# A gated mix of a spectral filter and a Mish layer: constants on another queue, Mish called first, half of the FFT result added on VectorE, and a new order

## The chip, the cores and the metric

The kernel runs on one core of a Trainium2 chip. The metric is device time in microseconds (us), the median of three runs; beside it stands one profiled execution with its own time and its span from the first to the last instruction.

## What is computed

```python
def reference(A_x, A_w_r, A_w_i, B_x, B_w1, B_b1, B_w2, gate_w):
    x = A_x                                             # (1, 2048, 512), bf16
    g = sigmoid((x * gate_w).sum(-1, keepdims=True))
    X = rfft2(x.astype(float32)) * (A_w_r + 1j * A_w_i)
    a = irfft2(X, s=(2048, 512)).astype(bfloat16)
    h = x @ B_w1 + B_b1                                 # 512 -> 1792
    b = (h * tanh(softplus(h))) @ B_w2                  # Mish, 1792 -> 512
    return g * a + (1 - g) * b
```

## The kernel before

The 2048 rows are 16 tiles of 128 rows (row p*16 + t belongs to tile t), in four chunks of four tiles. All work is a graph of named tasks. A written list, ORDER, names every task once; each engine, and each DMA queue, runs its own tasks in the order of that list. A token is name:engine:slot. The engine is given where several could do the task; the slot is the PSUM bank (of eight; tasks with pairs take two) or the temporary (of three). A task waits for its data and for all users of the slot's last owner. So order and slots are fixed by hand or by a planner outside the kernel, and TensorE never runs ahead of a task that waits. DMAs are in the lists too: most are issued by SP, a few by ScalarE (ACT) between its own instructions.

The tasks, with the lines of the profile:

- Loads (L462): x0, x2, x4, x8, x12 (tiles from that number on, 256 or 512 KB), w1_0, w1_4, w1_8, w2_2, w2_8, w2_0 (weights of the two layers), wr and wi pieces (spectral weights, named by half and piece: wi0s1), cRF and cFD (transform constants, both kept where w2's first two blocks come later), ldM and ldG (c_m and c_g, constants of the row transform), xt8 to xt15 (tiles transposed by the DMA, L461).
- tr0 to tr7: transposes of x tiles on TensorE (L560), copied to xT by evx (L492 on VectorE, L495 on ScalarE). tr_b does it for the bias and gate vectors (braw, graw).
- FFT forward: bf adds and subtracts the halves of x (L573), p (L586, needs cRF), its evacuation ep, d (L601, needs cFD and all p), its evacuation ed, then sixteen DMAs s (rE from rD, after all ed), then t (L716) and its evacuation et.
- Filter, in eight groups q: sw swaps halves (L726 VectorE, L727 ScalarE), p1, p2 and ad multiply and add (L734, L737, L740). The spectral weights are spread by wrm and wim (L640 ACT, L642 and L643), wrn and win (L660, L653), and small tasks wrc, wic, wrz, wiz. An edge column goes through e1 (L756), es, xp, ead, e2, e3.
- FFT backward: it (L794) and its evacuation eit, eight DMAs hx (rC from rF), id (L838), ec (L845, L846) and ey (L849), which leave yb, the result without its last matmul.
- First layer: m c_f (chunk c, block f; four 512-column matmuls, L864) and the Mish h c_f on ScalarE (L869). Chunks 2 and 3 write into rD and rS, so h2 waits for the s DMAs and h3 for all wrm and wim.
- Second layer: n t (fourteen matmuls, L882). In the kernel before, every n is followed in the same bank by ip (L890), the last FFT matmul, with constants RFs that are already scaled by exp of the gate's argument; o (L896, L899) scales the sum by omg = 1 - g. The scaled constants come by gate, zcl, ez (a power on POOL, L698), ezb, zt (L815), zte, the DMAs zw and zr through HBM, and rfs (L821).

The parameter merge says for how many tiles the FFT part is instead added behind the second layer: for t below merge, n has no ip in its bank, ip goes to a bank of its own with unscaled constants, and fin computes

```python
e.scalar_tensor_tensor(out=bs[:, t, :], in0=bank(b), scalar=gcol[:, t:t + 1],
                       in1=bs[:, t, :], op0=ALU.mult, op1=ALU.add)
```

on VectorE, after o; gcol is g, computed by one more small task, gc. Before, merge is 0. Results go out in pairs of tiles (out1, out3 and so on).

Of the kernel before, what the change touches and what calls it, by code (L numbers as in the profile page):

```python
# [9 lines left out]
F32 = mybir.dt.float32  # L10
AF = mybir.ActivationFunctionType
# [312 lines left out]


ORDER = """
warm::0 ebase ones graw x0 ident wrp0 wrp1 cRF x2 braw w1_0 tr1::0 bf0_0:dve bf0_1:dve tr0::1 evx1:act x4 p0::2 evx0:dve tr2::0 bf2_1:dve tr3::1
bf2_0:dve evx2:act p1 evx3:dve tr_b::4 x8 p2::6 p3 ep0:dve m0_0::5 ep2:act ev_b m0_2::1 ldM1 h0_0 bf4_1:dve tr7::0 h0_2 tr6::4 evx7:dve m0_3::5 wi0s2
bf4_0:dve evx6:act x12 tr4::1 bf8_1:dve h0_3 p6::6 p4::2 bf8_0:dve p5 evx4:act p7 tr5::5 xt11 ep4:act ep6:dve m0_1::4 cFD p8::0 p9 w1_4 evx5:dve h0_1
p10::6 p11 gate0::5 ep8:act bf12_1:dve bf12_0:dve m1_2::4 wi0s1 ep10:act zcl0 wip1 p12::0 ez0 h1_2 p14::2 p13 p15 ezb0 wip0 ep12:act m1_0::6 ez10 wi0s0  # L330
ep14:dve m0_6::7 h1_0 wr0s1 omg0 d6::2 h0_6 d7 d14::0 d15 ed6:act d10::4 ed14:dve d0::6 d1 wr0s0 d11 ed0:act m0_7::2 wim011:dve wr0s2 ed10:act d12::0
wim010:dve d13 d4::6 w1_8 d5 ed12:act wim001:dve m1_5::3 ed4:dve d2::4 h0_7 d3 wrm011:pool d8::0 h1_5 d9 ldM0 m1_6::2 ed2:dve ed8:act m1_7::3 h1_6 s1_1
wrm000:dve m1_4::0 wrm010:act s1_3 wim000:dve s0_3 m0_9::2 wrm001:dve s1_0 m0_11::1 win0:dve h1_4 s1_2 h1_7 m0_12::4 s0_1 wrn0:dve h0_11 s0_0 m1_10::3
h0_9 ldM3 h0_12 wic0:dve t3_0::0 t3_1 h1_10 wiz0:dve wrc0:pool t2_0::6 s3_3 et3:dve t2_1 m0_8::4 et2:act s3_1 m0_13::5 wrz0:dve s0_2 sw3_1:dve:0 h0_8
sw2_1:dve:1 s3_0 m1_13::6 sw3_0:dve h0_13 s3_2 sw2_0:dve p2_3:dve m0_5::7 wi1s0 h1_13 p2_2:dve t1_0::4 xt9 h0_5 t0_0::0 p1_3:dve t0_1 m1_1::6 et0:act
p1_2:dve wi1s1 ad_3:dve t6_0::2 t6_1 h1_1 t7_0::0 sw0_0:dve:2 t7_1 et6:act m0_10::7 ad_2:dve xt8 sw0_1:dve et7:act t1_1 sw6_0:dve:1 m1_9::6 p2_0:dve
h0_10 wr1s0 m1_3::0 sw7_0:dve:0 h1_9 p1_0:dve s2_2 m1_11::1 et1:act wim100:dve xt10 ad_0:dve m1_8::6 wim111:act sw6_1:dve m1_12::7 sw1_0:dve:2 wr1s1
sw1_1:dve wim101:dve m0_4::4 h1_12 p1_1:dve s2_3 h1_8 m2_3::5 wim110:dve s2_1 h1_11 m2_13::6 h0_4 p2_1:dve s2_0 h1_3 win1:dve ldM2 m2_8::7 m2_6::4 xt14
wrm101:dve wrm110:act m2_10::0 ad_1:dve h2_8 edge wrm100:dve m2_9::1 h2_13 xt15 wrm111:dve m2_7::7 h2_10 wic1:dve h2_6 wrn1:dve xt12 m2_1::0 h2_7 h2_3
m2_12::4 sw7_1:dve xt13 h2_1 wrc1:dve t4_0::6 wrz1:dve wiz1:pool t4_1 h2_12 t5_0::2 p2_6:dve t5_1 et4:act ldG1 m2_2::0 p2_7:dve p1_7:dve et5:act  # L340
m2_0::4 rft sw4_1:dve:2 inv m2_11::5 h2_9 sw4_0:dve ad_7:dve w2_8 h2_0 m3_5::1 p1_4:dve sw5_0:act:0 p2_4:dve m3_10::4 h2_11 sw5_1:dve ldG0 m3_8::2
p1_6:dve h3_5 h3_10 ad_4:dve m2_4::1 h3_8 ldG2 ad_6:dve m3_4::4 h2_2 p2_5:dve h2_4 p1_5:dve m3_3::5 ldG3 h3_4 ad_5:dve m3_12::1 h3_3 w2_2 e1::0 m3_7::5
h3_12 xp1::0 es0::1 m3_2::1 es1 h3_7 xp2 gate8::0 ead::2 h3_2 e2::5 m2_5::1 zcl8 e3 ez8 it0_0::4 ez18 h2_5 it0_1 ezb8 omg8 it6_0::2 zt::0 it4_0::6
eit0:act zte it6_1 it4_1 zw eit6:dve it3_0::0 it3_1 eit4:act it1_0::4 it1_1 eit1:dve eit3:act it7_0::2 it7_1 it5_0::6 zr it5_1 eit7:act it2_0::0 w2_0
eit5:dve it2_1 m3_0::4 eit2:act m3_13::5 h3_0 hx0_01 rfs m3_6::0 h3_13 hx0_11 hx0_00 m3_11::1 h3_6 hx0_10 m3_9::5 h3_11 hx4_00 m3_1::4 hx4_11 h3_9
id0::0 h3_1 hx4_10 id1 id2::6 ec0:act:2 id3 hx4_01 ec2:act:0 ey0_1 ey2_1 ey0_0 n0_0::4 ey2_0 n2_0::5 id8::6 id6::0 id9 n3_0::2 ec8:dve:0 ey8_0 ey8_1
ip3_0 id12::6 o3_0:dve id13 id7 ec12:act:0 n1_0::3 ec6:act:2 ey12_1 ey6_1 ey6_0 ey12_0 id10::0 id11 ip1_0 ec10:act:0 id14::6 o1_0:dve n6_0::2 ey10_0
ey10_1 ip6_0 ip0_0 o6_0:act ip2_0 o0_0:dve n8_0::0 o2_0:act out1 out3 n9_0::1 n7_0::5 ip8_0 n11_0::4 o8_0:dve id15 n10_0::0 ec14:act:0 ey14_1 ey14_0
n12_0::6 ip7_0 ip12_0 o7_0:act ip11_0 o12_0:dve id4::2 id5 o11_0:act n15_256::7 out7 ec4:act:0 ey4_0 ip9_0 ey4_1 n5_0::6 o9_0:act out9 ip10_0 ip15_256
ip5_0 o10_0:dve o15_256:act n4_0::1 o5_0:act out15_256 out11 n13_0::0 ip13_0 ip4_0 o13_0:dve n14_0::6 o4_0:act out13 out5 ip14_0 n15_0::7 o14_0:act  # L350
out14 ip15_0 o15_0:act out15_0
"""


def _build(nc, A_x, A_w_r, A_w_i, B_x, B_w1, B_b1, B_w2, gate_w, out, merge=0, xtp=8, NWARM=13):
# [8 lines left out]
    G = _Graph(3)  # L364
    es = ExitStack()
    with es:
        def sb(name, shape, dt):
            return es.enter_context(nc.sbuf_tensor(name, shape, dt))
# [48 lines left out]
        cst = w2_sb[:, 0, :]  # L417
        RF = w2_sb[:, 1, 0:128]
# [30 lines left out]
        def new_sem(name):  # L449
            return es.enter_context(nc.semaphore(name))  # L450
# [171 lines left out]
        for ri, (dstv, nm) in enumerate(((Wr, "wr"), (Wi, "wi"))):  # L622
# [3 lines left out]
            for fh in range(2):  # L626
# [5 lines left out]
                      writes=[(nm, fh, "p")], deps=dp)  # L632
# [180 lines left out]
        if merge < NT:  # L813
# [8 lines left out]
                out=RFs[:, merge:NT, :], in0=RFs[:, merge:NT, :], in1=RFT.unsqueeze(1).to_broadcast([128, NT - merge, 128]), op=ALU.mult))],  # L822
# [147 lines left out]
```

## Time and profile before

| | |
|---|---|
| runs | 145.08, 145.98, 146.22 us; median 145.98 |
| profiled execution | 145.54 us, span 143.8 us, mean granted clock 0.975 |
| TensorE | 130.7 us busy (91%), 918 matmuls |
| weight load / VectorE / ScalarE / POOL | 72.1 / 74.7 / 78.0 / 7.7 us |
| DMA | 20.67 MB, 144 GB/s on the mean |

The slices of the span are 3.6 us each, one digit per slice, in tenths. A line of the waits gives an instruction, what it waited for, the sum in us, how often, and the longest. The chain is the series of work that ended last, in order of time: start, length, what. Matmuls overlap, so the spacing in a run of them, not the mean duration of one, is what a matmul takes.

### The profile page before, as it was taken

To read this page: it belongs to the slowest core of one execution; us is meant where nothing else is said; L and a number is where in the kernel's file an instruction comes from. 1 tells how busy PE (TensorE), PEld (TensorE's weight loads), DVE (VectorE), ACT (ScalarE), POOL (GpSimd) and SP (SyncE) were. 2 spreads that over 40 slices of the span, in tenths; PEclk is the share of its full clock that TensorE was granted. 3 is DMA by queue.
4 is the path that set the end of the run, shared out by engine and by line. 5 is a ranking of instruction groups with operands and counts; after the bars stand their busy time and mean duration, and the time that the engine had idled before them with its cause. 6 is when DMAs were issued, how large, how long until landed. Compare 5 with 4: busy or idle time off the path is not lost.

```text
span 143.8 us, 2316 instructions
## 1 busy us (share of the span) xinstructions
PE 130.7 (91%) x918; PEld 72.1 (50%) x918; DVE 74.7 (52%) x125; ACT 78.0 (54%) x107; POOL 7.7 (5%) x16
## 2 busy tenths in 40 slices
PE   7499963999969999899997999999999999999992
PEld 5356733864526434353466645555444444644451
DVE  0566740799795999989736626067520212222100
ACT  3269970699966997999968973003130010412021
POOL 3000230050100000000022000000000000000000
PEclk9959998699999999999999999999999999999999
DMA  4999997006999989559980667000030000122031
GB/s 116 326 417 212 189 209 294 9 0 146 220 271 130 187 133 234 147 168 318 319 305 1 219 271 310 7 0 0 5 143 5 0 0 0 58 92 91 0 146 55
DMA packets 15710, 20.67 MB, mean 144 GB/s; under 512 B 5780, under 2 KB 11796, under 8 KB 15636
## 3 DMA queue, kind: packets, MB, share of 16 engines
q1 hardware_dynamic: 15232, 20.30, 53.2%
q10 hardware_dynamic: 468, 0.23, 0.6%
q8 instruction: 7, 0.11, 0.4%
q14 instruction: 3, 0.02, 0.1%
HBM read 13.19 MB, written 2.10 MB: 106 GB/s over the span
## 4 chain that ended last, share of the span: by engine, by line
PE 57%; DVE 14%; ACT 12%; DMA 10%; issue 3%; POOLq 1%; ACTq 0%; POOL 0%
PE ps L882 34%; PE ps L864 10%; DMA w_sb<-c_front 10%; ACT hs L869 4%; DVE tmp L726 3%; PE ps L838 3%; ACT rD L495 3%; PE ps L890 2%; PE ps L601 2%; DVE rC L740 2%; DVE tmp L737 2%; PE ps L794 1%; DVE rC L734 1%; ACT rW L640 1%; PE ps L716 1%
## 5 line engine op out<-in xcount | busy, mean ns | idle before, releaser
L864 PE MATMUL ps<-rX,w_sb 128*128 128x512 bf16 x224 | 52.8, 384 | 1.2 <-ACT rD L869 0.4
L864 PEld LDWEIGHTS ps<-rX,w_sb 128*128 128x128 bf16 x224 | 21.1, 99 | 26.0 <-issue 2.3
L882 PE MATMUL ps<-w_sb,hs 128*128 128x512 bf16 x112 | 25.3, 379 | 0.0
L899 DVE TENSOR_SCALAR rX<-ps,omg 128x512 bf16<-128x512 f32 x7 | 5.3, 750 | 25.5 <-PE ps L890 25.5
L869 ACT ACTIVATE hs<-ps,b1f 128x512 bf16<-128x512 f32 x28 | 17.9, 691 | 0.9 <-PE ps L864 0.5
L896 ACT ACTIVATE rX<-ps,omg 128x512 bf16<-128x512 f32 (+1 forms) x10 | 6.1, 642 | 21.4 <-PE ps L890 21.4
L845 ACT ACTIVATE tmp<-ps 128x512 f32<-128x512 f32 x7 | 4.0, 596 | 24.2 <-PE ps L838 24.1
L882 PEld LDWEIGHTS ps<-w_sb,hs 128*128 128x128 bf16 x112 | 10.8, 98 | 12.1
L849 DVE TENSOR_TENSOR rA<-tmp,ps 128x512 bf16<-128x512 f32 x16 | 10.1, 682 | 8.0 <-ACT tmp L845 7.9
L495 ACT ACTIVATE rC<-ps 128x1024 bf16<-128x1024 f32 x12 | 12.2, 1052 | 3.1 <-PE ps L716 1.9
L882 PE MATMUL ps<-w_sb,rS 128*128 128x512 bf16 (+1 forms) x70 | 12.9, 336 | 0.0
L882 PE MATMUL ps<-w_sb,rD 128*128 128x512 bf16 x56 | 12.6, 379 | 0.0
L869 ACT ACTIVATE rS<-ps,b1f 128x512 bf16<-128x512 f32 x14 | 9.4, 692 | 0.9 <-PE ps L864 0.9
L869 ACT ACTIVATE rD<-ps,b1f 128x512 bf16<-128x512 f32 x14 | 8.7, 710 | 1.9 <-PE ps L864 1.9
L882 PEld LDWEIGHTS ps<-w_sb,rS 128*128 128x128 bf16 x70 | 6.8, 98 | 5.5
L601 PE MATMUL ps<-w_sb,rC 128*128 128x128 bf16 x64 | 5.7, 264 | 3.7 <-DMA w_sb<-c_front 3.7
L882 PEld LDWEIGHTS ps<-w_sb,rD 128*128 128x128 bf16 x56 | 5.4, 98 | 6.4
L573 DVE TENSOR_TENSOR rB<-rA 128x1024 bf16<-128x1024 bf16 (+1 forms) x10 | 5.4, 578 | 4.9 <-DMA rA<-in_A_x_dram 4.9
L495 ACT ACTIVATE rD<-ps 128x1024 bf16<-128x1024 f32 x5 | 4.9, 1024 | 5.2 <-PE ps L601 5.2
L601 PEld LDWEIGHTS ps<-w_sb,rC 128*128 128x128 bf16 x64 | 5.3, 121 | 4.7 <-issue 4.2
L726 DVE COPY tmp<-rC 64x1024 bf16<-64x1024 bf16 x15 | 6.1, 420 | 1.8 <-ACT rC L495 1.4
L586 PE MATMUL ps<-w_sb,rB 128*128 128x128 bf16 x64 | 5.2, 236 | 1.9 <-DMA w_sb<-c_front 1.9
(79 smaller groups left out, 126.3 us busy)
## 6 DMA issues: line engine op xcount, KB each, us to landing
w_sb<-in_B_w_dram SPq DMA_DIRECT2D x3, 768.0 KB, 10.5
rF<-c_m SPq DMA_DIRECT2D x4, 512.0 KB, 8.1
rE<-rD SPq DMA_DIRECT2D x16, 128.0 KB, 4.7
rB<-c_g SPq DMA_DIRECT2D x4, 512.0 KB, 7.9
out_dram<-rX SPq DMA_DIRECT2D x7, 256.0 KB, 2.1
rA<-in_A_x_dram SPq DMA_DIRECT2D x3, 512.0 KB, 7.2
rC<-rF SPq DMA_DIRECT2D x4, 384.0 KB, 4.2
w_sb<-in_B_w_dram SPq DMA_DIRECT2D x2, 512.0 KB, 7.2
```

The lines of the kernel that those rows point to most:

```text
L495: return e.activation(o(), i(), AF.Copy)
L573: return e.tensor_tensor(out=xu[:, a:b_, uv, :], in0=x_sb[:, a:b_, 0:256], in1=x_sb[:, a:b_, 256:512], op=ALU.add if uv == 0 else ALU.subt ...
L586: ins = e.matmul(bank(b, i)[:, 128 * c:128 * (c + 1)], xu[:, t, uv, e_:256:2], RF, start=True, stop=True)
L601: ins = e.matmul(o_, zu[:, c, g, :], FD[:, c, :], start=True, stop=True)
L726: G.add(f"sw{q}_{j}", [("dve", 0.37, lambda e, z=z, lo=lo, i_=i_: e.tensor_copy(out=tb(z)[lo:lo + 64], in_=i_)), ("act", act(1024), lambda ...
L838: ins = e.matmul(bank(b, uv)[:, o:o + 128], Dv[:, uv, t, e_, :], cinv[:, 2 * uv + e_, :], start=True, stop=True)
L849: return e.tensor_tensor(out=yb[:, t:t + 2, 256 * h:256 * h + 256].rearrange("p t (i e) -> p t i e", e=2), in0=t4(z), in1=o4(bank(b, 1)), ...
L864: ins = e.matmul(bank(b), w1_sb[:, dt_, 128 * ft:128 * (ft + 1)], xT[:, c, dt_, :, :], start=(dt_ == 0), stop=(dt_ == 3))
L869: G.add(f"h{c}_{ft}", [("act", act(512, 1), lambda e, c=c, ft=ft, b=b: e.activation(hs[c][:, ft, :], bank(b), AF.Mish, bias=b1f[:, ft:ft + ...
L882: ins = e.matmul(bank(b)[:, 0:hi - lo], hs[c][:, ft, 128 * tl:128 * (tl + 1)], w2_sb[:, ft, lo:hi], start=(ft == 0), stop=(ft == NFT - 1 a ...
L896: return e.activation(bs[:, t, lo:hi], bank(b)[:, 0:hi - lo], AF.Copy, scale=omg[:, t:t + 1])
L899: return e.tensor_scalar(out=bs[:, t, lo:hi], in0=bank(b)[:, 0:hi - lo], scalar1=omg[:, t:t + 1], scalar2=None, op0=ALU.mult)
```

## The change

Five things are edited. cRF and cFD lose queue="act" and so go to SP's queue, where the x tiles are. A new task lut calls Mish once on a constant column, ahead of all other ScalarE work but one DMA issue. merge becomes 8, so that tiles 0 to 7 get ip in a bank of their own and a fin each, and zr and rfs handle 8 tiles instead of 16. ORDER is rewritten.

```diff
-def _build(nc, ..., merge=0, xtp=8, NWARM=13):
+def _build(nc, ..., merge=8, xtp=8, NWARM=13):
...
+        lut = sb("lut", [128, 1], F32)
...
+        G.add("lut", [("act", 1.3, lambda e: e.activation(lut[:, :], nc.const_aps.tensor(1.0, [128, 1], F32), AF.Mish))], "small", writes=["lut"])
...
-        dma("cRF", RF, d_front[:, 0, :], 0.2, writes=["cRF"], queue="act")
+        dma("cRF", RF, d_front[:, 0, :], 0.2, writes=["cRF"])
...
-        dma("cFD", cst, d_front[:, 1:5, :].rearrange("p c m -> p (c m)"), 0.5, writes=["cFD"], queue="act")
+        dma("cFD", cst, d_front[:, 1:5, :].rearrange("p c m -> p (c m)"), 0.5, writes=["cFD"])
```

The new order, cut to the places that matter (the start; the weights' second half; the edge; the end of the first layer and the start of the second):

```diff
+warm::0 braw wrp1 x4 ones lut ident wrp0 cRF ebase graw x0 w1_0 tr7::0 bf4_1:dve x2 tr4::1 bf4_0:dve tr5::2 wi0s0 evx4:dve tr0::3 bf0_1:pool evx5:dve
+tr_b::1 evx7:dve p6::4 evx0:act wr0s2 p7 ev_b p4::6 bf0_0:dve tr6::3 x12 ep6:dve p5 evx6:act p0::0 p1 tr1::2 ep4:act m1_3::3 ep0:dve bf2_0:pool x8
+evx1:act tr2::6 m1_1::7 h1_3 bf2_1:dve wr0s0 evx2:act p2::2 p3 h1_1 tr3::6 m1_0::0 ep2:act evx3:dve wr0s1 bf12_0:dve m0_3::1 h1_0 bf12_1:dve m1_2::2
+h0_3 bf8_0:dve w1_4 bf8_1:dve p14::6 h1_2 p15 p12::0 m0_0::3 wip1 ep14:act wip0 cFD p8::4 ldM2 h0_0 p9 gate0::6 ep8:act wrm010:dve p13 p10::2 ldM1 zcl0
...
+h1_9 t4_0::0 ad_0:dve t4_1 t5_0::2 h0_12 t5_1 sw3_0:dve m1_13::5 s3_0 sw2_1:dve:1 et5:act sw2_0:dve s3_3 m0_1::4 p1_3:dve et4:act wr1s1 p1_2:dve
+m2_6::2 h0_1 p2_2:dve h1_13 m2_8::3 wr1s0 p2_3:dve h2_6 ad_2:dve t7_0::4 m2_2::0 h2_8 wi1s0 ad_3:dve sw4_0:dve:1 t7_1 h2_2 m2_12::3 sw4_1:dve wi1s1
+sw5_0:dve:2 et7:act m2_1::2 sw5_1:dve ad_1:dve h2_12 t6_0::4 m2_0::0 sw7_0:dve:0 h2_1 ldG3 wrm111:dve t6_1 h2_0 m2_3::2 sw7_1:dve wrm100:dve rft
+et6:act m2_10::3 wrm101:dve xt14 h2_3 m2_7::4 wrm110:dve h2_10 xt15 wim110:dve wrn1:act m2_11::5 wim100:dve m2_13::3 xt13 wim111:dve m2_5::2 wim101:dve
...
+p1_6:dve ldG2 h2_5 m3_3::7 p2_6:dve h3_13 gate8::2 h3_3 ad_5:dve h3_7 m3_9::3 ad_6:dve zcl8 e1::6 ez8 m3_10::2 h3_9 xp1::1 ezb8 es0::2 ez18 zt::3
+m3_5::7 omg8 es1 zte h3_10 xp2 zw m3_0::6 ead::0 h3_5 e2::2 m3_6::7 h3_0 e3 w2_0 it4_0::2 h3_6 it4_1 zr it2_0::4 it2_1 eit4:act m3_12::6 eit2:dve
+it0_0::0 h3_12 it0_1 it3_0::2 it3_1 eit0:act it6_0::4 it6_1 n5_0::6 eit6:act rfs eit3:act it1_0::2 o5_0:dve it1_1 it5_0::4 it5_1 eit1:dve it7_0::0
+it7_1 n2_0::6 eit7:dve eit5:dve n1_0::7 hx0_01 o2_0:dve hx4_11 hx0_11 hx0_10 hx0_00 n3_0::6 hx4_01 o1_0:act hx4_00 hx4_10 id0::4 o3_0:act id1 id2::0
...
```

Before, x0 and x2 were the first loads, the second layer began behind the whole first layer with the hx DMAs already under way, and wrn1 ran on VectorE.

More of the change, by code (lines that the diff above doesn't have):

```diff
@@ L326 @@
 ORDER = """
[L327 to L350, printed above, removed]
@@ L351 @@
-out14 ip15_0 o15_0:act out15_0
+warm::0 braw wrp1 x4 ones lut ident wrp0 cRF ebase graw x0 w1_0 tr7::0 bf4_1:dve x2 tr4::1 bf4_0:dve tr5::2 wi0s0 evx4:dve tr0::3 bf0_1:pool evx5:dve
+tr_b::1 evx7:dve p6::4 evx0:act wr0s2 p7 ev_b p4::6 bf0_0:dve tr6::3 x12 ep6:dve p5 evx6:act p0::0 p1 tr1::2 ep4:act m1_3::3 ep0:dve bf2_0:pool x8
+evx1:act tr2::6 m1_1::7 h1_3 bf2_1:dve wr0s0 evx2:act p2::2 p3 h1_1 tr3::6 m1_0::0 ep2:act evx3:dve wr0s1 bf12_0:dve m0_3::1 h1_0 bf12_1:dve m1_2::2
+h0_3 bf8_0:dve w1_4 bf8_1:dve p14::6 h1_2 p15 p12::0 m0_0::3 wip1 ep14:act wip0 cFD p8::4 ldM2 h0_0 p9 gate0::6 ep8:act wrm010:dve p13 p10::2 ldM1 zcl0
@@ new lines @@
+wrm000:pool ep12:dve p11 m0_2::4 ep10:act m0_7::5 wi0s1 h0_2 wrm001:dve d4::2 h0_7 d5 d10::0 wrm011:dve d11 ed4:act d0::6 ldM3 d1 ed10:dve m0_6::5 ez0
+ed0:act d2::2 m1_4::4 ldM0 wrn0:dve h0_6 m1_7::6 h1_4 ez10 w1_8 wrc0:dve d3 omg0 wrz0:pool h1_7 d8::4 ezb0 gc0 d9 m1_6::7 ed2:act d6::0 ed8:act d7
+m0_4::6 wi0s2 ed6:dve h1_6 xt12 d14::4 d15 h0_4 d12::2 d13 ed14:act m1_5::0 ed12:dve xt9 m0_5::1 h1_5 wim001:dve s0_1 m1_10::2 h0_5 wim011:dve s3_2
+m0_9::3 wim010:dve s0_3 h1_10 s0_2 m1_8::1 wim000:pool h0_9 s0_0 m1_12::0 h1_8 s1_1 s2_1 m0_8::3 h1_12 win0:dve s2_3 m1_11::2 h0_8 s1_3 t1_0::0
@@ new lines @@
+wic0:pool s1_0 h1_11 t1_1 t0_0::4 wiz0:pool et1:dve s1_2 t0_1 m0_10::3 et0:act xt10 m0_13::2 sw1_0:dve:0 h0_10 sw0_0:dve:1 s3_1 m0_11::4 sw0_1:dve
+h0_13 sw1_1:dve s2_0 p2_0:dve t3_0::0 h0_11 t3_1 s2_2 t2_0::2 p2_1:dve t2_1 et3:act m1_9::5 xt8 p1_1:dve et2:act p1_0:dve m0_12::4 xt11 sw3_1:dve:2
+h1_9 t4_0::0 ad_0:dve t4_1 t5_0::2 h0_12 t5_1 sw3_0:dve m1_13::5 s3_0 sw2_1:dve:1 et5:act sw2_0:dve s3_3 m0_1::4 p1_3:dve et4:act wr1s1 p1_2:dve
+m2_6::2 h0_1 p2_2:dve h1_13 m2_8::3 wr1s0 p2_3:dve h2_6 ad_2:dve t7_0::4 m2_2::0 h2_8 wi1s0 ad_3:dve sw4_0:dve:1 t7_1 h2_2 m2_12::3 sw4_1:dve wi1s1
@@ new lines @@
+sw5_0:dve:2 et7:act m2_1::2 sw5_1:dve ad_1:dve h2_12 t6_0::4 m2_0::0 sw7_0:dve:0 h2_1 ldG3 wrm111:dve t6_1 h2_0 m2_3::2 sw7_1:dve wrm100:dve rft
+et6:act m2_10::3 wrm101:dve xt14 h2_3 m2_7::4 wrm110:dve h2_10 xt15 wim110:dve wrn1:act m2_11::5 wim100:dve m2_13::3 xt13 wim111:dve m2_5::2 wim101:dve
+w2_8 m2_4::0 win1:dve m2_9::1 h2_11 wrc1:dve h2_4 wic1:dve inv m3_8::6 h2_9 wiz1:dve wrz1:pool ldG0 p1_5:dve m3_4::5 h2_13 p1_4:dve h3_8 ldG1 m3_2::3
+p2_4:dve h2_7 p2_5:dve m3_7::6 h3_4 edge ad_4:dve h3_2 m3_1::7 p2_7:dve w2_2 sw6_0:act:1 p1_7:dve m3_11::3 h3_1 sw6_1:dve m3_13::5 ad_7:dve h3_11
@@ new lines @@
+ec0:dve:0 id3 n0_0::7 ec2:act:1 ey0_0 ey0_1 ey2_0 ey2_1 id4::4 o0_0:act ip0::0 id10::2 id11 ip1::1 fin0 ec10:act:1 id14::6 id15 id5 fin1 ec14:act:0
+n6_0::0 ec4:act:2 ey10_0 out1 ey14_0 ey14_1 ey10_1 ey4_1 id8::6 o6_0:act id9 id6::2 ey4_0 n11_0::1 ec8:act:1 ey8_1 ey8_0 ip3::0 ip11_0 fin3 id7
+o11_0:act n14_0::6 ec6:act:1 ey6_1 ey6_0 ip7::7 ip14_0 id12::2 o14_0:dve n4_0::1 out14 ip6::6 o4_0:act n10_0::0 fin6 ip10_0 ip2::6 o10_0:act ip4::1
+fin2 n7_0::4 out11 fin4 out3 n15_256::6 o7_0:act fin7 ip15_256 id13 out7 o15_256:act n8_0::7 ec12:dve:1 out15_256 ey12_1 ey12_0 ip8_0 n13_0::6 o8_0:act
@@ L352, with _build @@
+ip13_0 n12_0::7 o13_0:act ip12_0 n9_0::6 o12_0:act out13 ip9_0 ip5::7 o9_0:act n15_0::2 fin5 out9 out5 ip15_0 o15_0:act out15_0
 """
-def _build(nc, A_x, A_w_r, A_w_i, B_x, B_w1, B_b1, B_w2, gate_w, out, merge=0, xtp=8, NWARM=13):
+def _build(nc, A_x, A_w_r, A_w_i, B_x, B_w1, B_b1, B_w2, gate_w, out, merge=8, xtp=8, NWARM=13):
     cs = _build_consts()
```

## The prediction

> **What bounds the kernel now.** I read the page's forty slices first, then the waits of TensorE, then the chain of waits in order of time, then groups and DMA issues for prices.
>
> Slices of the span, 3.6 us each:
>
> ```profile
> PE   7499963999969999899997999999999999999992
> PEclk9959998699999999999999999999999999999999
> DMA  4999997006999989559980667000030000122031
> ```
>
> TensorE is nearly full from the tenth slice on. It is thin only in slices 1 to 2 and 6 to 7; behind each of those the granted clock has a bad slice (5 and 6 tenths). Who is waited for, TensorE's waits:
>
> ```profile
> PE ps L601 <- DMA w_sb<-c_front: 3.7, 1, 3.7
> PE ps L586 <- DMA w_sb<-c_front: 1.9, 1, 1.9
> PE ps L716 <- ACT hs L869: 1.7, 1, 1.7
> ```
>
> The two largest waits are for the two loads of transform constants, cFD (L601, the d tasks) and cRF (L586, the p tasks). The chain says when, and marks the stations that I use below (start, length, what):
>
> ```profile
> 1.40 4.82 DMA w_sb<-c_front
> ...
> 7.79 0.98 PE ps L586 x8
> ...
> 13.88 10.04 DMA w_sb<-c_front
> 23.92 0.14 issue
> 24.05 3.16 PE ps L601 x28
> ...
> 37.24 1.05 PE ps L716 x16
> ...
> 71.53 0.00 PE ps L756
> ...
> 80.29 5.18 PE ps L864 x24
> 85.47 0.21 issue
> ...
> 141.28 0.47 ACT rX L896
> ```
>
> So three stages: start to the t tasks (37.24), t to the edge task e1 (L756, 71.4), e1 to the end (143.8). From 37 to 71 the windows view shows three engines equally loaded (length, then busy of PE, PEld, DVE, ACT, POOL):
>
> ```profile
> 37.20:71.40 34.20, 31.37 (x190) 15.22 (x191) 30.36 (x53) 30.70 (x42) 0.58 (x2) 1.00 0.98 210
> ```
>
> Prices, from groups and DMA issues (a group ends in busy us, mean ns):
>
> ```profile
> L869 ACT ACTIVATE hs<-ps,b1f 128x512 bf16<-128x512 f32 x28 | 17.9, 691 | 0.9 <-PE ps L864 0.5
> L640 ACT ACTIVATE rW<-rS 32x2064 bf16<-32x2064 bf16 x2 | 3.9, 1930 | 0.0
> L727 ACT ACTIVATE tmp<-rC 64x1024 bf16<-64x1024 bf16 x1 | 1.1, 1055 | 0.2 <-DVE rC L740 0.2
> L869 ACT ACT_TABLE_LOAD x1 | 1.3, 1283 | 0.0
> L899 DVE TENSOR_SCALAR rX<-ps,omg 128x512 bf16<-128x512 f32 x7 | 5.3, 750 | 25.5 <-PE ps L890 25.5
> w_sb<-c_front ACTq DMA_DIRECT2D x1, 128.0 KB, 10.0
> w_sb<-in_B_w_dram SPq DMA_DIRECT2D x1, 256.0 KB, 4.1
> ```
>
> TensorE's unit prices come from the chain: a 512-column matmul is 0.216 us (24 in 5.18), so an m block of four is 0.863; a p, d or t matmul is 0.0656 (16 in 1.05), at the bad clock 0.113 to 0.12 (28 d in 3.16, 8 p in 0.98). The bad clock behind the cFD wait thus cost 1.3 us (3.16 against 28 x 0.0656). All 918 matmuls stay, so only gaps and slow clock can be won.
>
> **Stage 1, start to t.** In the new SP order the loads are x4, cRF, x0, w1_0, x2, wi0s0, wr0s2, x12, x8, wr0s0, wr0s1, w1_4, cFD, then c_m, wi0s1 and w1_8. Landings before (issue plus time to landing): x0 3.84, x2 5.99, w1_0 7.4, x4 8.7, x8 9.8, the first c_m load 11.2; so 512 KB takes 1.1 to 1.4 us in the stream, and the 250 KB w_i and w_r pieces 1.3 to 2.0 (17.1, 18.4, 20.0, 21.5). x4 first is bounded by x0's 3.84 and by x0 plus x2, the same bytes, 5.99: I take 5.25. Adding up: x0 6.5, x2 8.7, x12 11.5, x8 12.8, wr0s1 15.8, cFD 17.7.
>
> TensorE's order then gives: tr7, tr4, tr5 (12 matmuls, 0.8) to 6.05; tr0 at x0, to 6.95; tr_b behind evx4, which stands behind two adds of 0.68 and its own 0.42 on VectorE, 7.05. The table load now comes first on ScalarE (1.28 at about 1.4, the small activation 0.27 by L765), so graw issues near 3.0; by the 1.3 of the smallest DMA and the 4.8 of cRF it lands at 4.3 to 7.8: 0 to 0.75 late, I take 0. The second table load (at 9.87) falls away. I let the clock be bad up to about 10.5 as before, since TensorE idles as long: 24 p matmuls and one transpose block at 0.12, to 10.5. Then at full clock 12 transposes 0.8, 40 p 2.6, gate 0.8 and eight m blocks 6.9: d starts at 21.6, against 24.05 with seven m blocks before. cFD, 17.7, has 3.9 us of cover; without it d would start as late as cFD lands and pay the 1.3 us of bad clock too. bf0_1 and bf2_0 on POOL have no row: 0.5 (a quarter of the 2064-element POOL row's 1.9) to 1.9; I take 1.0; their users come at 10 and 12.7 while x0 and x2 land at 6.5 and 8.7, so either end is hidden.
>
> Behind d's start: 64 d matmuls 4.2, and among them 20 m matmuls 4.3, to 30.1; then eight m blocks, 6.9, to 37.0. The sixteen rE loads wait for the last d evacuation (1.23, to 31.4); before, it took 5.3 from that point (31.93) to t, so 36.7: just covered. Result: t starts at 37.0 as before, but with 84 m matmuls done instead of 64. The stage wins 20 x 0.216 = 4.3 and 0.2.
>
> Two rules of the skill bear on this. The cFD row: issued on ScalarE's queue at 13.88 it landed at 23.92, while w1_8, issued on SP at 13.47, landed at 25.1. The Trainium skill (DMA: Bandwidth & Descriptors, "Queues, rings and completion order") says an engine takes turns between queue rows; a small load on a row of its own would then be served early, and moving it behind SP's backlog would be a loss. The row shows no such favour, so I count place in the order alone; by the rule the move would cost up to what the backlog ahead of it costs, still inside the cover. The clock row: bad behind slice 1, where TensorE waited only 0.6 and 1.9 us. The Trainium skill (TensorE: Matmul & The Clock Gate, "Why this matters for your kernels") warns of gaps over about 3 us; by that the bad stretch of the front would not come at all, and the sum would be 1.3 us lower (24 p matmuls at 0.0656). The row decides, so I keep it.
>
> **Stage 2, t to e1.** TensorE: 120 m matmuls 25.9, 64 t 4.2, gate8 0.9: 31.0, to 68.0. VectorE, from t1's evacuation at 37.55: 1.23, 15 swaps (L726) at 0.44, 24 products and sums (L734, L737, L740) at 0.705, eight copies (L642, L643) at 0.72, win1 1.26, small ones 0.76: 32.5, to 70.1. ScalarE: seven evacuations at 1.03, 30 Mish at 0.64 (0.60 back to back, 0.69 alone), one swap 1.06, and wrn1, which is new there: 64x4160, bounded by the line through the two rows shown (0.84 ns an element: 3.7) and by L727's rate (4.3); nearest L640, 3.9. From 38.1 this is 31.4, to 69.5, plus the wait of wrn1 for the copies wrm on VectorE (done at 56.2, ScalarE there at about 55): 70.7. Behind wrn1 stand h2_11, h2_4, h2_9 and the m3 activations; six m blocks have free banks meanwhile, then m3_2 waits for h2_13 and gate8 for h2_5. The multiplicands for it (wr1, wi1 loads) now come behind fourteen rE loads and five transposes, issued 45.5 to 48; at 5 to 7 us to landing they are in time for 53.6 and 56.2. The transposes xt11 and xt13 (2.7 to 3.1 landing when the queue is quiet) land at about 46 and 59.5, for m blocks at 47 and 60.4. I take e1 at 70.6, with 204 m matmuls done against 188.
>
> **Stage 3, e1 to the end.** Before: 72.4 us. Four m blocks and gate8 are already done: 3.45 and 0.9 less. The wait for zt (0.6) grows by 0.3, since ezb8 hangs on POOL's 1.65. Then n5 comes early, with w2_0 behind zw: zte 72.9, zw landed 1.3 later, w2_0 issued 74.5, landing 4.1: 78.6, with n5 at 78.7 (it had 3.7 us to spare before). The rC loads start behind the last rF copy at 86.5; the fifth, wanted by id0, lands about 5 later (0.6 per issue, 2.0 to 2.7 landing); n1 and n3 cover until 92.5. fin0 to fin7 are new on VectorE: between L849's 0.68 and L492's 1.22, by L899 0.75, 6.0 in all, hidden in the 25.5 us that VectorE waits there for TensorE; rfs halves. Without that cover each would cost its 0.75. The separate ip matmuls were there before. Sum: 72.4 - 4.35 + 0.3 = 68.4.
>
> Span: 70.6 + 68.4 = 139.0, against 143.8. The profiled execution's own time was 145.54, 1.74 above its span; so 140.7. The median of the runs, 145.98, stands 0.44 above the profiled one; I say 141.0.
>
> **Rivals.** First, the middle stage is TensorE's alone: e1 at 68.0, time 138.4. For it: VectorE had small waits in its chain that a new order may hide. Against: 32.5 of listed work. Second, the wr1 and wi1 loads land late: before, loads behind transposes and rE pieces took 7.3 to 8.2; at the 10 us seen in the front they land at 57, VectorE and wrn1 stand 3.4 us longer: 144.4. Third, slower: n5 takes the wait that cFD gave up. If w2_0 is not on a quiet queue, the 768 KB loads' 6.8 to 10.5 apply; at 10.5 n5 starts 6.3 late and a stretch of bad clock (1.3) follows: 148.6. It is slower than before beyond 1% from a landing of 9.3 us on (6.4 over my 141.0, of which 1.3 is the clock). For it: cover of 0.1 us only. Against: all other large loads are issued by 61.5. That the change does not do what it says, cFD still landing last near 24, would cost 2.4 and 1.3 of clock: 144.7; it is counted with the second.
>
> **How the numbers follow.** The forecast (139 to 143.5) 0.57; the first rival 0.12; late loads 0.18; n5's wait 0.13. Range 137.5 to 146.0, which takes in x4's 0.7 either way, graw's 0.75, wrn1's 0.4, and leaves out n5's wait and a little below. A measurement of this kernel can tell about 1%, 144.5 to 147.4: faster takes the forecast, the first rival and about half of the late loads, 0.79; same 0.08; slower 0.13.
>
> **What would show it.** Right: L603 no longer waits for c_front; the clock row has no second bad slice; t starts near 37, e1 near 70.6; fin on L914 near 0.75. Wrong: a wait of L884 for w_sb, a bad clock slice behind slice 3, L758 later than 73, or L603 after 24.

## The result and the profile after

The changed kernel takes 136.61 us (median of four runs, 135.21 to 137.92); the kernel before took 145.53 beside it. The ratio is 0.943, with a 95% interval of 0.926 to 0.960. Run again on another chip it took 137.75 against 144.66, 0.962 (0.952 to 0.972). These comparisons leave out runs well above a kernel's fastest, so a stretch of bad clock that comes in some runs only is hardly seen in a ratio, and I give medians beside it. The profiled execution took 137.92, with a span of 136.2.

The prediction, 141.0 and faster, had the direction right, but 136.61 lies below its range, 137.5 to 146.0.

The forty slices after, 3.4 us each:

```profile
PE   7499999999998699999989999999999999999992
PEclk9959999999999999999999999999999999999999
DMA  4999999996876899579923100780200102220024
```

Of the two stretches of bad clock one is left, in the front. The hole that stood in slices 6 and 7 is gone; a thin place stands at slices 13 and 14 (45 us), and the DMA row is still full up to slice 9. TensorE's waits (total, times, longest, in us):

```profile
PE ps L562 <- DMA rA<-in_A_x_dram: 1.8, 2, 1.4
PE ps L866 <- DMA rX<-in_A_x_dram: 1.2, 1, 1.2
...
PE ps L817 <- DVE ezb L701: 0.7, 1, 0.7
PE ps L718 <- ACT rC L496: 0.5, 1, 0.5
```

No line names c_front any more. What is left are transposes that wait for x4 and x0 (L562, at 5.2 and 6.4), one m block that waits for the transposed tile xt11 (L866, at 46.6), zt's wait for ezb, and a run of t tasks at 42.7 that waits for ScalarE to empty a bank. The chain of waits, in order of time (start, length, what):

```profile
6.41 11.00 DMA rS<-in_A_w_r_dram
...
21.27 1.34 PE ps L603 x24
...
55.46 3.67 ACT rW L665
...
67.35 1.20 DVE rC L742 x2
68.55 0.09 DVE zcl L698
...
75.46 1.34 PE ps L796 x24
76.85 2.97 PE ps L884 x13
...
90.22 0.89 PE ps L840 x16
...
133.63 0.47 ACT rX L898
```

The d tasks (L603) run at full clock, n5 (76.85) starts straight behind the it tasks, and id0 (90.22) straight behind n3. Between t (35.90) and e1 (68.72), the windows view (length, busy of PE, PEld, DVE, ACT, POOL, then clock, DMA share and GB/s), one DMA issue and one group:

```profile
35.90:68.72 32.82, 30.77 (x214) 15.72 (x217) 29.86 (x54) 29.71 (x40) 0.95 (x3) 1.00 0.83 217
```

```profile
w_sb<-c_front SPq DMA_DIRECT2D x1, 128.0 KB, 12.2
```

```profile
L914 DVE SCALAR_TENSOR_TENSOR rX<-ps,gcol,rX 128x512 bf16<-128x512 f32 x8 | 5.8, 748 | 21.5 <-PE ps L910 17.9
```

By stages, with m blocks (0.86 each) and gate8 (0.79) put where they now stand, the span's 7.6 us come from here:

| stage | before | after | work moved | won |
|---|---|---|---|---|
| start to t | 37.24 | 35.90 | five m blocks more, 4.3 | 5.7 |
| t to e1 | 34.12 | 32.82 | one block less, gate8 more: 0.1 less | 1.2 |
| e1 to the end | 72.44 | 67.48 | four blocks and gate8 less, 4.2 | 0.7 |

### The profile page after: what moved, and what is told of

It is laid out like the page before. It is cut to its first block, busy times and chain, and to the rows that moved or that the text cites. A ratio compares the mean times of both kernels' runs of the same rounds, so it can differ in the third digit from the quotient of the medians.

```text
span 136.2 us, 2309 instructions
## 1 busy us (share of the span) xinstructions
PE 127.2 (93%) x902; PEld 71.2 (52%) x918; DVE 77.6 (57%) x129; ACT 76.7 (56%) x107; POOL 13.1 (10%) x21
## 4 chain that ended last, share of the span: by engine, by line
PE 56%; ACT 13%; SPq 12%; DMA 11%; DVE 3%; issue 2%; POOLq 1%
PE ps L884 35%; SPq L463 10%; PE ps L866 10%; DMA rS<-in_A_w_r_dram 8%; DMA rX<-in_A_x_dram 3%; ACT rD L871 3%; ACT rW L665 3%; PE ps L840 3%; PE ps L796 3%; ACT rD L496 2%; SPq L462 2%; ACT hs L871 2%; DVE rC L742 1%; PE ps L892 1%; PE ps L910 1%
## 5 line engine op out<-in xcount | busy, mean ns | idle before, releaser
L866 PE MATMUL ps<-rX,w_sb 128*128 128x512 bf16 x215 | 50.9, 380 | 2.0 <-DMA rX<-in_A_x_dram 1.2
L866 PEld LDWEIGHTS ps<-rX,w_sb 128*128 128x128 bf16 x224 | 20.9, 98 | 23.4 <-issue 2.1
L898 ACT ACTIVATE rX<-ps,omg 128x512 bf16<-128x512 f32 (+1 forms) x14 | 9.2, 657 | 42.3 <-PE ps L884 23.8
L884 PE MATMUL ps<-w_sb,hs 128*128 128x512 bf16 x108 | 24.8, 379 | 0.2
L871 ACT ACTIVATE hs<-ps,b1f 128x512 bf16<-128x512 f32 x28 | 18.9, 690 | 3.0 <-PE ps L866 2.7
L914 DVE SCALAR_TENSOR_TENSOR rX<-ps,gcol,rX 128x512 bf16<-128x512 f32 x8 | 5.8, 748 | 21.5 <-PE ps L910 17.9
L884 PE MATMUL ps<-w_sb,rD 128*128 128x512 bf16 x53 | 12.3, 379 | 0.2
L851 DVE TENSOR_TENSOR rA<-tmp,ps 128x512 bf16<-128x512 f32 x16 | 10.0, 682 | 1.1 <-ACT tmp L847 1.1
L575 DVE TENSOR_TENSOR rB<-rA 128x1024 bf16<-128x1024 bf16 (+1 forms) x8 | 4.8, 637 | 6.3 <-DMA rA<-in_A_x_dram 6.3
L493 DVE CAST rC<-ps 128x1024 bf16<-128x1024 f32 x4 | 4.9, 1218 | 1.3 <-PE ps L588 0.7
L493 DVE CAST rF<-ps 128x1024 bf16<-128x1024 f32 x4 | 4.7, 1218 | 1.3 <-PE ps L796 1.3
L742 DVE TENSOR_TENSOR rC<-rC,tmp 128x1024 bf16<-128x1024 bf16 x8 | 5.3, 688 | 0.1
L496 ACT ACTIVATE rX<-ps 128x512 bf16<-128x512 bf16 x4 | 2.4, 595 | 5.3 <-PE ps L562 5.3
```

What stands on the lines that cost most here:

```text
L493: return e.tensor_copy(out=o(), in_=i())
L496: return e.activation(o(), i(), AF.Copy)
L742: return e.tensor_tensor(out=Y[:, fa:fb, :], in0=Y[:, fa:fb, :], in1=zv(z), op=ALU.add)
L851: return e.tensor_tensor(out=yb[:, t:t + 2, 256 * h:256 * h + 256].rearrange("p t (i e) -> p t i e", e=2), in0=t4(z), in1=o4(bank(b, 1)), ...
L866: ins = e.matmul(bank(b), w1_sb[:, dt_, 128 * ft:128 * (ft + 1)], xT[:, c, dt_, :, :], start=(dt_ == 0), stop=(dt_ == 3))
L871: G.add(f"h{c}_{ft}", [("act", act(512, 1), lambda e, c=c, ft=ft, b=b: e.activation(hs[c][:, ft, :], bank(b), AF.Mish, bias=b1f[:, ft:ft + ...
```

## The experiments

**The constants' queue.** Two kernels: the kernel before with cRF and cFD on SP's queue, and the changed kernel with both back on ScalarE's.

```diff
 before_const_on_sp (in the kernel before)
-        dma("cRF", ..., writes=["cRF"], queue="act")
-        dma("cFD", ..., writes=["cFD"], queue="act")
+        dma("cRF", ..., writes=["cRF"])
+        dma("cFD", ..., writes=["cFD"])
 after_const_on_act (in the changed kernel): the reverse
```

> The kernel before with one part of the change: both constant loads go to SP's queue, at the places that its own order gives them (cRF between x0 and x2, cFD between the first transposed tile and w1_4). Theory A (the place of cFD in the stream is most of the gain): cFD lands near 14 to 16, d starts at 20.4 instead of 24.05, no wait of L601 for c_front, no bad clock slice behind it; 3.7 + 1.3 us off, 140.0 to 141.5 us. Rival B (the new order as a whole makes the gain, this part is taken back behind by VectorE and ScalarE): within 1% of before, 144 to 147 us.

> The changed kernel with this one part undone: cRF and cFD on ScalarE's queue, order unchanged. Theory A (place in the stream decides): cRF is issued behind lut at about 3 and lands at about 7.8, cFD behind ep14 at about 17.5 and lands 8 to 10 us later, behind c_m and w1_8; d waits about 5 us and a bad clock stretch follows: 142.5 to 144.5 us. Rival (a queue of its own is served in turn with SP's): cFD lands 2 to 3 us after its issue, near 20.5, and the time stays at 136 to 137.5 us.

Before with SP's queue: 141.55 against 145.49, ratio 0.966 (0.956 to 0.976). After with ScalarE's queue: 142.32 against the same 145.49; the changed kernel's variants that differ only in the warm-up took 137.2 and 137.9 on that chip. So the queue alone is worth 3.9 us in the old order and 4.5 to 5.1 in the new one: about half or more of the whole gain on that chip (7.6 to 8.3). From TensorE's timeline and the DMA issues of the first kernel, and then the waits and DMA issues of the second:

```profile
19.29 1.96 PE L601 MATMUL ps<-w_sb,rC 128*128 128x128 bf16 x32
...
31.22 1.05 PE L716 MATMUL ps<-rE,rF 128*128 128x128 bf16 x16 [0.32 <-ACT hs L869]
...
37.62 0.83 PE L716 MATMUL ps<-rE,rF 128*128 128x128 bf16 x12 [1.90 <-issue]
```

```profile
w_sb<-c_front SPq DMA_DIRECT2D x1, 128.0 KB, 6.9
```

```profile
PE ps L603 <- DMA w_sb<-c_front: 3.2, 1, 3.2
```

```profile
w_sb<-c_front ACTq DMA_DIRECT2D x1, 128.0 KB, 7.8
```

In the first, no d task waits. d starts at 19.3 instead of 24.05, and 32 d matmuls take 1.96 where 28 took 3.16. So t starts 6.0 us earlier, and e1 and the end come 5.8 earlier. Little is given back in this trace: the wait of 1.9 at a later run of t tasks (37.6) stood in the kernel before too (1.7, at 43.5). The median gains only 3.9. The profiled run, at full clock, is the fastest of four; the other three show a mean clock of 0.976 to 0.988. In the second the wait of the kernel before is there again: ScalarE reaches cFD's issue only at 16.6, the load needs 7.8, and d starts at 24.5. Of its four runs the one at full clock took 139.7, so 1.8 to 2.5 us are lost without a stretch of bad clock. The gain is thus the moment of issue. A queue of its own does not make up for it. What of the rest of the gain belongs to the new order and what to merge isn't measured apart.

**Wait or clock?** Thirty matmuls on constants fill most of TensorE's wait for cFD in the kernel before.

```diff
 before_fill (in the kernel before)
+        G.add("fill", [("pe", 30 * 0.107, f_fill)], "warm", writes=[flb])   # 30 matmuls, 256 columns, bank 5
 ORDER: ... -d6::2  +fill::5 d6::2 ...
```

> The kernel before, with 30 matmuls of 256 columns on constants between the first layer's block and d6, where TensorE waits 3.7 us for cFD; they fill 3.2 us of that wait (30 at 0.107) and change nothing else. It parts the price of cFD's late landing into the wait and the slow clock behind it. Theory A: the bad clock (28 d matmuls in 3.16 us instead of 1.6) follows from TensorE standing idle; filled, d still starts at 24, but the bad slice is gone, t comes 1.3 to 1.6 us earlier, and the time is 1.3 us (0.9%) below before. Rival B: the slow slice is there whether TensorE is idle or not: within 0.4% of before, the slice is seen still at 24 to 27. In both the wait itself stays, so that of the 3.9 us that the other queue wins at least 2.3 are the wait.

The chain of this kernel:

```profile
23.14 1.74 PE ps L611 x28
```

The 28 d matmuls take 1.74 us where they took 3.16, and no stretch of bad clock is left in the trace; its price in this place was 1.4 us, close to the 1.3 summed. One trace can't show that it followed from the idle engine, since the stretch in the front is gone from it too, where nothing was edited. The mean clock of the single runs says more: one such stretch is 0.012 of it, and 10 of the 12 filled runs stood at 0.998 or more, against 3 of the 18 runs before, which carried none to three. So filling the wait takes away about one stretch per run. Yet the time is 144.08 against 144.73, ratio 1.004 (0.999 to 1.009): no difference shown. The ten filled runs at 0.998 or more took 142.8 to 145.15, the three of before 142.4 to 143.95, so at the same clock the filled kernel is no faster. Both theories had a half right: theory A the trace, rival B the time. Filling gains 0.65 by medians where the other queue gains 3.9 (on another chip). That the larger part is the wait itself fits the 4.8 by which d came earlier there, but isn't measured apart.

**Warm-up, table load, place of wrn1.** Four small edits in the changed kernel:

```diff
 after_warm20:      -NWARM=13  +NWARM=20
 after_warm4:       -NWARM=13  +NWARM=4
 after_no_lut:      -        G.add("lut", ...)        (and lut out of ORDER)
 after_wrn1_on_dve: ORDER: -wrn1:act  +wrn1:dve
```

> The changed kernel with 20 warm-up matmuls instead of 13, so that TensorE is busy until about the landing of x4 (5.2). Theory A (the idle stretch ahead of x4 brings the bad clock slice of the profiled execution, in some executions and not in others): no bad slice, span 134 to 135, and a median up to 0.7 us below the changed kernel's. Rival (the bad slice comes from the small gaps between 5.2 and 10, or at random): a bad slice as often as before, same time.

> The changed kernel with 4 warm-up matmuls instead of 13, so that TensorE idles from about 1.8 to 5.2. Theory A: the bad slice comes in all executions, 24 p matmuls, transposes and the first m blocks take twice as long: 1.3 us or more longer than the changed kernel, 137.9 to 139 us. Rival (warm-up does not matter, the DMA stream sets the start of d at 21 anyway): same time within 0.5 us.

> The changed kernel without the early Mish call: a second table load of 1.28 us comes back at the first h. Theory A (ScalarE waits over 5 us in the front anyway, and m blocks have banks): up to 0.4 us longer. Rival (it stands on the path): 1.3 us longer, 137.9 us.

> The changed kernel with the copy of 64x4160 back on VectorE. Theory A (VectorE sets e1, from t to the last sum without a gap): 1.25 us more on VectorE, e1 0.9 to 1.25 later: 137.5 to 138 us. Rival (ScalarE's 3.7 us block sets the Mish activations and so TensorE): e1 same or earlier, 136.6 us or less.

Measured: 137.85 and 137.21 with the warm-ups (ratios 0.946 and 0.943), 137.93 without the early Mish (0.968 on a chip where the changed kernel had 0.962), 138.12 with wrn1 on VectorE (a chip on which the changed kernel itself was not run). None differs from the changed kernel by more than its own runs do (136.3 to 139.7). Of the warm-up neither effect of the theories came; the time stays, as the rivals have it, and d starts at 20.7 and 19.9. Without the early Mish it is 0.2 more than the changed kernel's on that chip, within theory A's 0.4 and within the noise. Of wrn1, the trace says more than the time: t to e1 is 32.87 against 32.82. VectorE works 1.24 us more there, and its waits for ScalarE of 0.7 (the swap) and 0.6 (an evacuation) are gone, so the two cancel. Neither the theory (e1 0.9 to 1.25 later) nor the rival's time (136.6 or less) came.

**The second layer's cover.** merge back to 0: ip again in n's bank, all sixteen scaled constants, and the tail of ORDER rewritten by me for it, which no planner has tuned.

```diff
 after_merge0
-merge=8
+merge=0
 ORDER, tail: -... n0_0::7 ... ip::0 ... fin0 ...   +... n0_0::4 ip3_0 ip2_0 o3_0:act o2_0:dve ...
```

> The changed kernel with merge back at 0: every tile gets its last FFT matmul in the bank of the second layer, and n5, n2, n1 and n3 hold banks 6, 7, 4 and 5 until it; the order up to the last rF copy is unchanged, behind it it is a new one written by hand. Theory A (adding on VectorE serves to let four tiles of the second layer run and give back their banks while the rC loads are under way): TensorE waits 2 to 3 us once behind id3 for ec and ey, the rest is the same: 138.5 to 140 us. Rival (the separate adds are not what covers the loads): within 1% of the changed kernel.

141.31 us (140.9 to 141.66), more than either theory said, beside a kernel before at 144.37. Stage 3 is 71.9 instead of 67.5. Its waits:

```profile
PE ps L892 <- DVE rA L851: 1.7, 1, 1.7
...
PE ps L884 <- ACT rX L898: 0.8, 1, 0.8
```

An ip (L892) stands in n's bank and waits for ey (L851); the banks come free later, so an n waits for an o (L898). A stretch of bad clock at 93.3 to 96.7 costs another 1.7 (half of 3.4). Together 4.2 of the 4.4. So fin is what lets n tasks stand ahead of the FFT's last steps in this order. But the 4.4 is not what merge gains in the change: the kernel before has merge 0 too, in an order made for it, and its stage 3 was only 0.7 longer than the changed kernel's on equal work.

**The price of a 128-column matmul.** In the changed kernel each id task does its four matmuls twice (the second time into the same place).

```diff
 after_id_twice
-                    for uv in range(2):
+                    for uv in (0, 1, 0, 1):
```

> The changed kernel with every id matmul (L840) issued twice, 64 more 128-column matmuls in the stage that TensorE alone bounds. Theory A (a 128-column matmul costs 0.0557 us; my 0.0656 had the time until the first result of a run of 16 in it): 64 x 0.0557 = 3.6 us longer, span 139.8 if the clock slice comes again, 0.223 per id task in the chain. Rival (0.0656 is the price, weight load included): 4.2 us longer.

140.2 us; stage 3 grows from 67.5 to 71.0, 3.5 for 64 matmuls, 0.055 each. The chain shows the spacing directly:

```profile
88.71 1.79 PE ps L840 x32
```

32 in 1.79 is 0.056. The rival's 0.0656, the price in my sum, falls.

**What else could be won.** The changed kernel once more, and five other orders of its tasks:

```diff
 after_again:       no edit
 after_xt_early:    ORDER: xt10 xt8 xt11 moved ahead of s0_1
 after_front:       ORDER: x12 x8 w1_4 cFD moved ahead of wi0s0; wrm010, wrm000 behind ep12
 after_gate8_early: ORDER: gate8::2 zcl8 ez8 moved ahead of h2_9 (as gate8::7), ezb8 ez18 omg8 behind p2_5, zt zte zw ahead of m3_9
 after_gate8_fixed: the same, with ez8 behind wrz1:pool
 after_gate8_front: after_gate8_fixed with the edit of after_front
```

> The changed kernel once more, so that the variants beside it have it on the same chip. Theory A (the stages do not depend on the execution, only the front does, by where the clock's first release falls): e1 to the end 67.4 to 67.6, t to e1 31.9 to 33.2, d at 19.8 to 21.1; 136 to 137.5 us. Rival (the profile that came with the result was off as a whole): other stages by over 1 us.

> The changed kernel with the transposed tiles xt10, xt8 and xt11 issued ahead of the sixteen rE loads, in a stretch in which SP's queue waits for the last d evacuation (25.2 to 30.5). Theory A (TensorE's wait of 1.2 us at m2_6 is xt11's place in the queue): the wait goes, t starts as before, e1 comes up to 1.2 us earlier where VectorE and ScalarE follow: 135.5 to 136.3 us. Rival (VectorE's chain sets e1): wait gone, e1 at 68.5, same time.

> The changed kernel with x12, x8, w1_4 and cFD ahead of the pieces of w_i and w_r in SP's queue, and the first two w_r copies behind ep12. Theory A (in the front x8's landing at 16 and w1_4's at 19.6, late by the 16 KB and 514 B rows of the w pieces, set bf8, p8 and m0_7): no wait of L588 or L866 for a load, d at 18.8 to 19.5, t 0.5 to 1.5 earlier, 135.2 to 136.2 us. Rival (what is won is lost at t, where the Mish activations and the rE loads hold it): t at 35 to 36, same time.

> The changed kernel with gate8, zcl8 and ez8 right behind m3_8, ezb8, ez18 and omg8 behind p2_5, and zt, zte, zw just ahead of m3_9: the power on POOL then runs under the filter, and TensorE's wait of 0.7 for ezb8 behind e1 goes. Theory A (that wait stands on the path, e1 does not move): e1 to the end 66.8 instead of 67.5, 0.7 us off the changed kernel. Rival (VectorE's chain sets e1 and takes the four small tasks on): e1 0.5 later, nothing won.

> The changed kernel with gate8 and its chain moved ahead by about 11 us, but with its power on POOL behind wrz1 instead of ahead of it. Theory A: the loss of the first move of gate8 (e1 at 72.9 instead of 69) came only from wrz1, and so from the products behind it; with the order on POOL mended e1 is back at 68 to 69, the wait of the zt matmuls for ezb (0.7) is gone, and the time is 0.5 to 1 us below the changed kernel's, a ratio to before 0.005 to 0.01 lower than its 0.943 to 0.962. Rival B: the gate's small matmuls and instructions cost as much wherever they stand, and zt's wait is only replaced: within 0.5 us of the changed kernel. Rival C: the loss had another cause, the bank that gate8 takes from the first layer: e1 stays at 72 or later and the ratio near 0.98.

> The same with x12, x8, w1_4 and cFD issued ahead of the spectral weights, which alone changed nothing. Theory A: the two edits touch different stages, so this is within 0.3 us of the kernel with the gate alone. Rival: the earlier d pays once the middle stage has no other wait, 0.5 to 1 us below it, a ratio to before near 0.935 to 0.945.

The kernel again: 137.75. In its trace t to e1 took 32.1 and e1 to the end 67.5, and only the front moved, as theory A has it: d at 21.8, somewhat past the range given for it. Transposes early: 138.17, nothing won. The wait for xt11 is gone and t to e1 takes 31.94, 0.9 less, but on SP's timeline (start, length, what) five DMA transposes stand in front of the s transfers:

```profile
18.38 12.48 SPq L462 DMA_TRANSPOSE rX<-in_A_x_dram  x5
30.98 1.20 SPq L463 DMA_DIRECT2D rE<-rD  x2
```

The last d evacuation ends at 29.3, but the s loads start only at 30.98, and t at 35.85: the d tasks had come 1.1 us earlier than in the changed kernel, and the queue took it. Loads early: 137.66 against 137.75, the same time. Its trace has d at 19.8 and t at 35.5, the trace of the kernel run beside it 21.8 and 37.5; but traces of the changed kernel's front without this edit have d anywhere from 19.8 to 21.9 and t from 35.1 to 37.6, so one trace can't tell the edit from that spread. Gate early: 140.22, ratio 0.982, slower than the changed kernel. VectorE's groups and TensorE's waits give the reason:

```profile
L736 DVE TENSOR_TENSOR rC<-rC,rW 128x1024 bf16<-128x1024 bf16 x8 | 5.2, 685 | 2.1 <-POOL rW L674 2.0
```

```profile
PE ps L866 <- ACT rS L871: 2.0, 1, 2.0
```

ez8 (2.03 us on POOL, the mean of its two) stood ahead of wrz1 (L674); p1 waited for it, everything of the middle stage behind that shifted, and e1 came at 72.9. With ez8 behind wrz1 e1 is back at 69.2, and zt's wait is 0.2 instead of 0.7: theory A has the cause of the loss right, and rival C falls. But the time is 138.14 (ratio 0.958, 0.949 to 0.966), and 138.17 with the loads early (0.963): no gain shows in the time. In the first one's trace e1 to the end takes 66.5, 1.0 less, but e1 now has a listed wait that it did not have.

```profile
PE ps L758 <- DVE rC L742: 0.6, 1, 0.6
```

The edge task waits for the last sum on VectorE (L742). No version is shown to beat the changed kernel.

## Why the prediction was right, and where it was wrong

| station | said | measured |
|---|---|---|
| x0 / x2 / x8 land | 6.5 / 8.7 / 12.8 | 6.3 / 9.9 / 16.1 |
| cFD lands | 17.7 | 20.0 |
| d starts | 21.6 | 21.1 |
| t starts | 37.0 | 35.9 |
| e1 | 70.6 | 68.7 |
| w2_0 lands / n5 | 78.6 / 78.7 | 75.3 / 76.85 |
| e1 to the end | 68.4 | 67.5 |
| span | 139.0 | 136.2 |
| profiled time | 140.7 | 137.9 |
| median | 141.0 | 136.6 |

**Right.** cFD's wait goes, and with it the second bad slice; twenty more m matmuls fit ahead of t; fin takes 0.748, hidden in VectorE's idle time; n5 and the id tasks find their data. The two kernels with the constants' queue changed show the first point to be worth about half of the gain or more. The first bad slice stayed in the profiled execution, as said. POOL's bf took 1.15 (said 1.0) and wrn1 3.67 (3.9, bounds 3.7 to 4.3).

**What failed.** The path held; three terms of the sum were mis-sized, and two waits of before were kept behind e1 that are gone. The terms are the price of a 128-column matmul (0.0656, measured 0.0557), the list of the middle stage (33.6 from t to e1, measured 32.8), and the step from the profiled time to the median (plus 0.44, measured minus 1.3). The front's loads were wrong too, the other way and without a price.

**Wrong: 2.8 us of span.** They fall as 0.5 up to d, 0.6 from d to t, 0.8 from t to e1 and 0.9 behind e1.

The first mis-sized term is the price of a p, d, t, it or id matmul. I took 0.0656 from "16 in 1.05", the t tasks at 37.24 in the chain of before. That length runs to the end of the last matmul, so it holds the time to a result once; the timeline of before has the next matmul 0.89 behind the first of the 16:

```profile
37.24 1.05 PE L716 MATMUL ps<-rE,rF 128*128 128x128 bf16 x16
38.13 3.62 PE L864 MATMUL ps<-rX,w_sb 128*128 128x512 bf16 x16
```

That is the spacing of 0.0557 (24 in 1.34, above); the other 0.16 is paid once where TensorE starts behind a wait, not for each matmul. For the 64 d matmuls the error is 64 x 0.0099 = 0.63, which is the 0.6 from d to t. For 40 p and 12 transposes at full clock it is 0.5; up to d this is net of loads that were later than said, so its share there isn't separated, and that d came within 0.5 of the forecast is in part luck. Behind e1 I had kept all of before's time but the work that moved. TensorE stopped there twice more in before, ahead of 24 it tasks and of the 16 id tasks:

```profile
PE ps L838 <- issue: 0.2, 1, 0.2
PE ps L794 <- DVE rF L492: 0.2, 1, 0.2
```

The new order has neither wait. With the 0.16 to the first result each cost nearly 0.4, together 0.7. The zt wait grew by less than 0.1 (0.63 to 0.66) where I added 0.3, and gate8 took 0.79 where I took off 0.9, 0.1 the other way. That is the 0.9.

From t to e1 the mechanism held. The chain runs through wrn1 on ScalarE and ends with VectorE's last sum at 68.55; e1 follows 0.17 behind it, as it does by 0.12 to 0.17 in the traces of the variants that keep gate8's place, and in gate8_fixed its wait for that sum is listed. The rival that TensorE alone sets e1 falls with this, and since e1 came 32.8 after t and not 31.0. The list was too dear: from its first evacuation to the last sum VectorE took 32.0, where I had added up 32.5, and I had put e1 0.5 behind that sum. Its rows had not changed from before (products 0.687 us, swaps 0.421); I had put 0.02 more on each, while two in a row took 1.20 and not 1.41 ("L742 x2" above). Together that is the 0.8. One wait I had put at nothing: xt11 landed at 46.4, near the 46 of my sum, but its m block was ready at 45.4 and not at 47, and TensorE stood 1.2 us. In xt_early, where that wait is gone, t to e1 is 31.94, so the wait hid a part of the error.

**Wrong: the step from the profiled time to the median.** I added 0.44, the distance of before's median from its profiled run. It should have been minus 1.3. The profiled execution after holds one stretch of bad clock (mean clock 0.987); the other three runs have none (1.0). The profiled execution before holds two, and its runs none to three. A stretch that isn't in every run has no fixed place between profile and median. This is 1.75 of the 4.4 us by which I missed, the largest single part, and no term of the kernel. That the stretch makes all of that 1.3 isn't shown: the changed kernel's runs at a mean clock of 0.999 or more still went from 135.2 to 139.7. Run again on the other chip, the kernel took 137.75, which is inside the range; so the last part of the miss is of the size of that difference.

**Wrong without a price: the front's loads.** x8 came 3.3 late and cFD 2.3, where I had added up 1.1 to 1.4 us for 512 KB and 1.3 to 2.0 for a piece of the spectral weights. Most of x8's came in one step: it landed 3.7 behind x12 (12.3, then 16.1). Two pieces of the spectral weights were under way with it; whether they took the time isn't settled. The cover for cFD was 1.1 and not 3.9; it sufficed. after_front, with those loads ahead, shows no gain in time.

The other rivals. Late wr1 and wi1 loads: no line of the waits names them. n5's wait: w2_0 was issued at 72.5, took 2.7 on a quiet queue, and had 1.6 us to spare; the slower side needed a landing of 9.3.

**Clock and queue.** The bad front stretch came in the profiled run though no single wait of TensorE for data passed 1.4 us there (before, where I wrote 0.6 and 1.9, the trace has 0.1 and 1.9). The Trainium skill (TensorE: Matmul & The Clock Gate, "Why this matters for your kernels") has a gap of about 3 us as what brings it; in this case shorter gaps brought it, and over all kernels it is there in some executions and not in others. With four warm-up matmuls a wait of 3.2 shows no stretch, but that trace has not yet been granted full clock there, so it is no counterexample. In kernels with the changed kernel's front, d came at 20.7, 21.1 and 21.8 where the stretch was there, and at 19.8, 20.0, 20.1, 20.4 and 21.9 where it was not: 0.8 apart on the mean, less than the spread, where I had put 1.3 on it. The last section says why this is no price of slow clock.

The Trainium skill (DMA: Bandwidth & Descriptors, "Queues, rings and completion order") would let a load on a queue row of its own be served in turn; cFD took 7.8 to 10.2 us on ScalarE's queue and 6.9 to 13.5 on SP's. No early service shows.

Open: the changed kernel's median moved by 1.1 between two chips, at the same granted clock, and none of these runs says why.

## What to carry to other kernels

Look for a small load that a busy engine issues late: it was worth about half or more of this change, and the gain was the moment of issue. Take a unit price from the longest run of a kind that stands in the middle of other work; a length in the chain that starts behind a wait holds the time to one result, which must be counted once. When a stretch of bad clock stands in a profile, see in how many of the timed runs it is before it becomes a term of the sum, and don't carry a distance of profile to median from one kernel to another.

## What was not expected of the hardware

The stretches of bad clock that end inside a trace were 3.41 us long in every one. Full clock was first granted at 3.5 to 4.2 us in some traces with SP's constants in the new order, and three of four of these had a bad stretch at 7 to 11; where it was first granted at 6.5 us or later, none had one there. But until that first grant the matmuls run at half speed, and the mean clock of a run does not count this: in xt_early, with a mean clock of 1.0, sixteen transposes took 2.09 us where twelve took 0.84 in the changed kernel's profile. The first line is the changed kernel's, the second xt_early's:

```profile
5.19 0.84 PE L562 MATMUL ps<-identt,rA 128*128 128x128 bf16 x12 [1.42 <-DMA rA<-in_A_x_dram]
4.98 2.09 PE L562 MATMUL ps<-identt,rA 128*128 128x128 bf16 x16 [1.20 <-DMA rA<-in_A_x_dram]
```

So the front has slow clock in either case, up to a late first grant or behind a short stretch of full clock; only the traces of after_no_lut and before_fill were spared. The traces also show what goes ahead of a stretch. Take the 13 traces that hold their first grant, and cut each into pieces of 3.41 us from there on: all eleven pieces in which TensorE stood idle for 2.0 us or more in sum were followed at once by a stretch (the one ahead of before's d tasks was idle for all 3.4), and none with 1.5 or less. Of five with 1.7 to 1.85 two were, the changed kernel's 1.7 at 4.0 to 7.4 among them. So idle time in sum within a piece went with it here, and not one long gap; where the pieces fall differs between executions.

The number of warm-up matmuls (4, 13, 20) did not show in the time. Five DMA transposes of x tiles occupied SP's queue for 12.5 us in the busy front, where one in the middle stage took 1.3; set ahead of the s transfers, they delayed them all.
